# A fused attention, MLP and gate kernel: token tiles 2 to 15 transposed by DMA rather than by TensorE and ScalarE

## The chip, the core, the metric

One core of a Trainium2 chip. The metric is the device time of one execution in microseconds; a kernel is run several times and its median is quoted. All runs told here were in the fast state. "Span" is the length of the one execution that the profiler recorded; it is about 1.8 us shorter than that execution's time. Engines in the profile: PE is TensorE, PEld its weight load, DVE VectorE, ACT ScalarE, POOL GpSimd, SP the queue that issues all DMA.

## The reference, cut

```python
# x: 2048 tokens x 1024, 32 heads of 32, F = 3584, all bf16
xn  = layernorm(x)
q, k, v = split_heads(xn @ wqkv)
s   = concat(softmax(q k^T / sqrt(32)) v) @ wo
g   = silu(gelu(layernorm(xn) @ w1 + b1) @ w2 + b2)    # tanh form of gelu
return x + s * g
```

## The kernel before

The whole block is one program. Attention runs as 512 "units": 8 groups of four heads, times 8 query blocks of 256 tokens, times 8 key pairs of 256. A unit is a score group of 8 matmuls, two exponentials of 128x1024 on ScalarE, 8 matmuls with V, and a row sum by ones-matmuls. All other matmuls (projections, the MLP for 8 chunks of 256 tokens, the output projection) are slipped between the score groups, through the two PSUM banks that attention leaves free. The order of each engine is made when the program is built, by a list scheduler in the kernel itself, with a small cost model (a duration for each instruction, a bandwidth for loads). On the chip every engine then follows its list, whatever really happens.

Start, for each token tile: statistics on VectorE, `pow` and the normalising pass on GpSimd, then the transpose:

```python
def tr_item(t, half=None):                       # eight 128x128 transposes on TensorE ...
    ...
        ins = e.transpose(bankb(b)[:, dc*128:(dc+1)*128], xnb[t % 4][:, dc*128:(dc+1)*128], ident[:])
    ...                                          # ... and a copy out of PSUM on ScalarE
        act(lambda e: e.activation(dst, src(), ACT.Copy), c_act(128 * n), [], W, 0, it)
...
for t in (lo, lo + 1):
    pool(... xnb[t % 4] = xst[t] * rs + nb ...)  # one pass over 128x1024
pro_q += [tr_item(lo), tr_item(lo + 1), k_pair_item(n, False)]
```

First layer of the MLP, one item of 512 columns:

```python
dve(... xb = psum + b1 ...); dve(... sq = xb * xb ...); dve(... ut = (sq + 1/GA) * xb ...)
act(lambda e: e.activation(ut_t[i3][:], ut_t[i3][:], ACT.Tanh, scale=GC * GA), c_act(512), ...)
dve(... h = (ut + 1) * xb ...)
```

Row sums over two units; the first NOPA units make no additions on VectorE and leave the summing to TensorE:

```python
NOPA = 24
def ones_pair(u, pv):
    pa = dve(... PA[u], PA[u+1] = P[.., 0, :] + P[.., 1, :] ...)   # 2048 wide
    pb = dve(... PA[u] += PA[u+1] ...)                             # 1024 wide
    ...
    if u < NOPA or u >= HG * 64 - 2: plan.skip.append(pa)
```

The cost model's view of a load, and of an issue on the queue:

```python
state["bw"] = max(state["bw"], t) + o.nbytes / 210.0     # bytes per ns
return add("SP", fn, 70, 0, R, W, prio, sem=sem, nbytes=nbytes, extra=extra)
```

## Time and profile before

| | before |
|---|---|
| median of 3 | 1062.07 us (1061.9 to 1062.5) |
| span of the profiled run | 1060.2 us |
| first exponential, 15th exponential | 12.7, 45.9 us |
| end of the last exponential | 1046.1 us |
| from there to the end (tail) | 14.1 us |
| 512-wide matmuls after the last exponential | 42 |

The prediction below shows the busy line, the chain and the stretches. Two more views matter later. The first line is the granted TensorE clock in 40 slices of the page; the others are the last pieces of the chain (start, length, instruction).

```profile
PEclk9999999999999999999999999999999999999999
...
1047.59 9.24 PE ps L668 x42
...
1056.86 0.70 DVE w1r L1221
...
1057.58 0.43 DVE w1r L1228
```

The clock is full in nearly all of the span: no slice is under nine tenths, but one stretch of 3.41 us, at 57.65 us, has half the clock. After the last exponential the chain is 42 left-over matmuls of the output projection in one run of 9.24 us, two short operations and a store. That line deserved more attention than it got: work of TensorE is left over when ScalarE has finished.

### The profile page before, as it was taken

The numbers are of one execution on the slowest core, as the hardware profiler recorded it, in microseconds if no ns is written. First come the engines' busy times: TensorE is split into PE (matmuls) and PEld (weight loads), VectorE is DVE, ScalarE is ACT, GpSimd is POOL, SyncE is SP. The second block draws the span as 40 slices with busy tenths as digits, with TensorE's granted clock in tenths as the row PEclk, the third lists the DMA queues.
The fourth block names the chain that finished last, engine by engine and source line by source line (L and its number), as shares of the span: only waits on it lengthen the run. The fifth ranks groups of instructions, "written<-read, shape, count | busy, mean of one in ns | idle before, by whom it ended". The sixth has DMA issues, their size and how long they took to land.

```text
span 1060.2 us, 32647 instructions
## 1 busy us (share of the span) xinstructions
PE 1026.5 (97%) x14502; PEld 643.7 (61%) x14562; DVE 946.9 (89%) x1585; ACT 1028.9 (97%) x1186; POOL 31.2 (3%) x42
## 2 busy tenths in 40 slices
PE   7999999999999999999999999999999999999998
PEld 5756466556665566566665566466665666665443
DVE  8479898999999998899989998999999998978996
ACT  4999999999999999999999999999999999999994
POOL 5500000000000000000000000000000000000000
PEclk9999999999999999999999999999999999999999
DMA  9335166522674466423763476224765776662442
GB/s 268 111 96 158 42 179 190 144 76 71 186 207 126 113 193 196 113 57 112 206 192 105 122 199 195 74 76 121 212 180 151 221 217 190 179 197 70 134 140 87
DMA packets 285798, 156.52 MB, mean 148 GB/s; under 512 B 23642, under 2 KB 276570, under 8 KB 285658
## 3 DMA queue, kind: packets, MB, share of 16 engines
q1 hardware_dynamic: 285658, 154.44, 51.0%
q8 instruction: 114, 1.87, 0.8%
q14 instruction: 26, 0.21, 0.1%
HBM read 142.35 MB, written 12.06 MB: 146 GB/s over the span
## 4 chain that ended last, share of the span: by engine, by line
ACT 93%; PE 4%; DVE 2%; DMA 1%; issue 0%; SPq 0%; POOL 0%; POOLq 0%
ACT P L1067 86%; ACT ut L939 5%; PE ps L668 3%; ACT gw L971 2%; DVE stats L823 1%; DMA hT<-in_A_x_dram 1%; PE ps L663 1%; ACT big L814 0%; PE ps L1058 0%; PE ps L803 0%; DVE yT L911 0%; POOL gw L847 0%; DVE V L740 0%; DVE mv L825 0%; SPq L693 0%
## 5 line engine op out<-in xcount | busy, mean ns | idle before, releaser
L1067 ACT ACTIVATE P<-ps 128x1024 bf16<-128x1024 f32 x1024 | 986.8, 1243 | 5.3 <-PE ps L1058 5.3
L1087 DVE TENSOR_TENSOR PA<-P 128x2048 bf16<-128x2048 bf16 x243 | 294.7, 1215 | 25.4 <-ACT P L1067 24.1
L668 PE MATMUL ps<-yT,w1r 128*128 128x256 bf16 x1792 | 234.9, 275 | 2.3 <-DVE xb L931 1.1
L668 PE MATMUL ps<-w2r,hT 128*128 128x256 bf16 x1792 | 226.9, 273 | 0.3 <-DVE nv L1121 0.2
L668 PEld LDWEIGHTS ps<-yT,w1r 128*128 128x128 bf16 x1792 | 162.1, 98 | 60.5 <-issue 28.6
L668 PEld LDWEIGHTS ps<-w2r,hT 128*128 128x128 bf16 x1792 | 162.2, 98 | 51.0 <-issue 30.5
L1091 DVE TENSOR_TENSOR PA<-PA 128x1024 bf16<-128x1024 bf16 x219 | 147.7, 684 | 1.4
L663 PE MATMUL ps<-P,V 128*32 128x256 bf16 x4096 | 142.8, 274 | 0.6 <-DVE xb L931 0.4
L668 PE MATMUL ps<-big,qk 128*128 128x512 bf16 (+2 forms) x522 | 120.9, 357 | 5.7 <-issue 2.1
L668 PE MATMUL ps<-qk,big 128*128 128x256 bf16 (+1 forms) x723 | 121.2, 305 | 2.5 <-issue 1.3
L663 PEld LDWEIGHTS ps<-P,V 128*32 128x32 bf16 x4096 | 97.7, 96 | 33.1 <-issue 19.6
L1058 PE MATMUL ps<-QKT 32*128 32x256 bf16 x2048 | 101.7, 273 | 7.4 <-ACT P L1067 5.9
L1058 PE MATMUL ps<-qk 32*128 32x256 bf16 x2048 | 101.9, 273 | 6.2 <-ACT P L1067 2.1
L939 ACT ACTIVATE ut<-ut 128x512 f32<-128x512 f32 x112 | 94.5, 855 | 0.0
L668 PEld LDWEIGHTS ps<-qk,big 128*128 128x128 bf16 x736 | 65.3, 98 | 41.5 <-issue 13.3
L931 DVE TENSOR_TENSOR xb<-ps,b1T 128x512 bf16<-128x512 f32 x112 | 76.6, 684 | 13.9 <-PE ps L668 12.6
L941 DVE SCALAR_TENSOR_TENSOR hT<-ut,xb 128x512 bf16<-128x512 f32 x112 | 76.4, 684 | 5.9 <-ACT ut L939 5.2
L668 PEld LDWEIGHTS ps<-big,qk 128*128 128x128 bf16 x568 | 47.7, 98 | 52.4 <-issue 15.6
L1058 PEld LDWEIGHTS ps<-QKT 32*128 32x128 bf16 x2048 | 30.3, 92 | 76.6 <-ACT P L1067 75.9
L937 DVE SCALAR_TENSOR_TENSOR ut<-sq,xb 128x512 f32<-128x512 bf16 x112 | 76.1, 682 | 0.3
L1058 PEld LDWEIGHTS ps<-qk 32*128 32x128 bf16 x2048 | 30.4, 92 | 71.6 <-ACT P L1067 67.4
L663 PE MATMUL ps<-PA,ones 128*32 128x256 bf16 x1068 | 56.0, 274 | 0.3 <-DVE PA L1091 0.3
(75 smaller groups left out, 532.2 us busy)
## 6 DMA issues: line engine op xcount, KB each, us to landing
w1r<-in_B_w_dram SPq DMA_DIRECT2D x112, 512.0 KB, 4.4
w2r<-in_B_w_dram SPq DMA_DIRECT2D x128, 448.0 KB, 4.4
qk<-in_A_wqkv_dram SPq DMA_DIRECT2D x16, 256.0 KB, 3.2
g_scratch<-gw SPq DMA_DIRECT2D x32, 128.0 KB, 3.0
o_scratch<-ot SPq DMA_DIRECT2D x56, 64.0 KB, 2.8
big<-o_scratch SPq DMA_DIRECT2D x28, 128.0 KB, 3.5
hT<-in_A_x_dram SPq DMA_DIRECT2D x10, 256.0 KB, 5.5
qk<-in_A_wqkv_dram SPq DMA_DIRECT2D x4, 512.0 KB, 4.4
```

The source lines that it names most:

```text
L663: ins = e.matmul(dst(j), lhsT=lhsT(j), rhs=rhs(j), start=start, stop=stop, tile_position=(0, 32 * j), skip_group_check=True)
L668: return e.matmul(dst, lhsT=lhsT, rhs=rhs, start=start, stop=stop, skip_group_check=True)
L823: dve(lambda e, t=t, c=c: e.bn_stats(stats[:, t, c, :], xst[t][:, c * 512:(c + 1) * 512]), 600, [XS(t)], [("st", t, c)], 1)
L931: dve(lambda e: e.tensor_tensor(xb_t[i3][:].rearrange("p (k t) -> p k t", k=2), bank(it.bank).rearrange("p (k t) -> p k t", k=2), b1T[:, 2 ...
L937: dve(lambda e: e.scalar_tensor_tensor(ut_t[i3][:], sq_t[p % 2][:], 1.0 / GA, xb_t[i3][:], op0=ALU.add, op1=ALU.mult), c_f32(512), [("sq", ...
L939: act(lambda e: e.activation(ut_t[i3][:], ut_t[i3][:], ACT.Tanh, scale=GC * GA), c_act(512), [("ut", i3)], [("ut", i3)], 1)
L941: dve(lambda e: e.scalar_tensor_tensor(hT[:, hs].rearrange("p k t -> p (k t)"), ut_t[i3][:], 1.0, xb_t[i3][:], op0=ALU.add, op1=ALU.mult), ...
L971: act(lambda e: e.activation(zh_t[zi], z_t[zi], ACT.Tanh, scale=0.5), c_act(512), [("z", zi)], [("zh", zi)], 1)
L1058: ins = e.matmul(bank(b0[j], kk * 256, (kk + 1) * 256), lhsT=QKT[sl][32 * j:32 * j + 32, 1, kb * 128:(kb + 1) * 128], rhs=QKT[sl][32 * j:3 ...
L1067: x = act(lambda e, h=h: e.activation(P[pi][:, 2 * h:2 * h + 2].rearrange("p j k q -> p (j k q)"), ps[:, pr[h] * 1024:(pr[h] + 1) * 1024], ...
L1087: pa = dve(lambda e: e.tensor_tensor(PA_all[:, a0:a0 + 2].rearrange("p u j q -> p (u j) q"), P_all[:, p0:p0 + 2, :, 0, :].rearrange("p u j ...
L1091: pb = dve(lambda e: e.tensor_tensor(PA[a0][:], PA[a0][:], PA[a1][:], op=ALU.add), c_b16(1024), [("PA", a1)], [("PA", a0)], PBPRIO)
```

## The change

The intent: take 14 copies off ScalarE and 112 transposes off TensorE in the start by transposing with DMA, and, in the same edit, make the tanh wider, the matmul chunks finer and the end shorter. The diff also changes nine other constants of the scheduler (GRACE1, GRACE2, HARD, EARLY, RESERVE, GLAST, OLAG, PJC and PJD), which set when it puts which work; no run sets these back alone. The diff cut to its core:

```diff
-NOPA = 24
+NOPA = 0
 ...          # other constants of the scheduler
+FINE = 1          # MLP and V matmuls may be interrupted after each, not after two
+PART = 5
+TD = 2            # tiles from 2 on: DMA transpose
 ...
-                state["bw"] = max(state["bw"], t) + o.nbytes / 210.0
-                o.fin = state["bw"] + 1900.0
+                state["bw"] = max(state["bw"], t) + o.nbytes / 280.0
+                o.fin = state["bw"] + (2600.0 if o.sem.startswith("tp") else 1900.0)
 ...
-            return add("SP", fn, 70, 0, R, W, prio, ...)
+            return add("SP", fn, 430, 0, R, W, prio, ...)
 ...
-            pro_q += [tr_item(lo), tr_item(lo + 1), k_pair_item(n, False)]
+            for t in (lo, lo + 1):
+                if t < TD:
+                    pro_q.append(tr_item(t))
+                else:
+                    add("SP", lambda e, t=t: e.dma_start_transpose(out=xnT[:, :, t * 128:(t + 1) * 128], in_=xnb[t % 4]),
+                        1500, 0, [("xnb", t % 4)], [("xnT", t, h) for h in range(2)], 0, sem=f"tp{t % 4}", nbytes=360000)
+            pro_q.append(k_pair_item(n, False))
 ...          # first w1 loads, later x loads and the third wq/wk load wait for tiles of the start
-            act(lambda e: e.activation(ut_t[i3][:], ut_t[i3][:], ACT.Tanh, scale=GC * GA), c_act(512),
+            act(lambda e: e.activation(ut_t[i2][:], ut_t[i2][:], ACT.Tanh, scale=GC * GA), c_acts(1024),
 ...
-        def ones_pair(u, pv):
+        def ones_four(u, pv):         # additions over four units: one ones-matmul group in place of two
 ...
+                if qb == PART:        # heads 0 to 6 of the last 256 tokens are projected early,
+                    ...               # head 7 alone is left for the end
+                            wo_item(NQB - 1, t2, nh, 0, 7)
```

> **What bounds the kernel now.** I read the page's busy line, then the chain of work that ended last, then stretches of the span, and only then single instructions.
>
> The busy line and the chain, from the page of the kernel before:
>
> ```profile
> PE 1026.5 (97%) x14502; PEld 643.7 (61%) x14562; DVE 946.9 (89%) x1585; ACT 1028.9 (97%) x1186; POOL 31.2 (3%) x42
> ...
> ACT 93%; PE 4%; DVE 2%; DMA 1%; issue 0%; SPq 0%; POOL 0%; POOLq 0%
> ...
> L1067 ACT ACTIVATE P<-ps 128x1024 bf16<-128x1024 f32 x1024 | 986.8, 1243 | 5.3 <-PE ps L1058 5.3
> ```
>
> Two engines stand at 97%, but the chain is ACT for 93% of the span: the 1024 exponentials of the softmax. Their mean of 1243 ns overlaps the neighbour; what one costs is the step from its start to the next start. The cost of the other ACT work shows in this timeline of ACT (start, length, instruction):
>
> ```profile
> 404.62 0.91 ACT L939 ACTIVATE ut<-ut 128x512 f32<-128x512 f32 x1
> 405.14 6.80 ACT L1067 ACTIVATE P<-ps 128x1024 bf16<-128x1024 f32 x7
> 411.58 0.87 ACT L971 ACTIVATE gw<-gw 128x512 f32<-128x512 bf16 x1
> 412.10 4.94 ACT L1067 ACTIVATE P<-ps 128x1024 bf16<-128x1024 f32 x5
> ```
>
> A 512-wide tanh costs 405.14 - 404.62 = 0.52 us. Over the trace the commonest step of an exponential is 0.904 us, the mean 0.915. The stretches show where ACT is not full:
>
> ```profile
> 12.70:46.00 33.30, 30.40 (x350) 24.10 (x349) 25.33 (x67) 26.75 (x29) 26.49 (x32) 1.00 0.65 185
> 46.00:967.00 921.00, 901.04 (x13021) 577.82 (x13067) 834.49 (x1362) 920.08 (x1069) 0.00 (x0) 1.00 0.52 148
> 967.00:1046.10 79.10, 75.42 (x988) 32.10 (x997) 71.01 (x119) 79.08 (x87) 0.00 (x0) 1.00 0.39 123
> 1046.10:1060.20 14.10, 10.56 (x80) 5.00 (x79) 7.41 (x15) 0.00 (x0) 2.31 (x2) 1.00 0.21 75
> ```
>
> (Columns: length, then busy time of PE, PE weight load, DVE, ACT, POOL, clock, DMA.) There are three regimes: a start until 46 us, in which units of attention wait for their token tiles; 1000 us with ACT continuously busy; and a tail of 14.1 us without any ACT. The account of the ACT regime: at 45.94 the 15th exponential starts; 1009 x 0.904 = 912.1, 144 tanh x 0.52 = 74.9 and the last one's 1.25 end at 1034.2. It really ends at 1046.1, so 12 us are small bubbles, nearly all ahead of the first exponential of a unit.
>
> In the start, ACT's copies of transposed tiles alternate with the exponentials:
>
> ```profile
> 33.55 3.77 ACT L814 ACTIVATE big<-ps 128x1024 bf16<-128x1024 bf16 x4 [0.35 <-PE ps L803]
> 37.18 1.97 ACT L1067 ACTIVATE P<-ps 128x1024 bf16<-128x1024 f32 x2
> 38.99 2.00 ACT L814 ACTIVATE big<-ps 128x1024 bf16<-128x1024 bf16 x2
> ```
>
> but POOL, which normalises the tiles, is as full (26.5 of 33.3 us, and 4.2 to 4.75 in each 5 us from 15 to 40). Its pairs of tiles are 3.56 us apart (rows at 20.43 and 23.99), and the last pair ends at 38.2.
>
> **What the skill says.** The Trainium skill, "ScalarE: Activation LUTs", section "What ACT_TABLE_LOAD costs": an ACTIVATE with immediate scale and bias takes 186 ns + 0.833 ns per column, and neighbours overlap by about 93 ns. The step would be 93 + 0.833N: 519.5 ns at N = 512, and the trace has 520. So for a 1024-wide tanh, which no trace here has yet, I estimate 946 ns from that formula. The skill's "DMA: Bandwidth & Descriptors", section "DMA Transpose (X-bar)", limits DMA transposes to 2-byte types and the Sync or Scalar queues; its section "Latency and other measured facts" gives an effective 261 GB/s, so a 256 KB tile is an estimated 1.0 us of transfer. No trace of before has one; plain 256 KB loads in the start needed 5.5 to 7.1 us from issue to landing in a busy queue, 2.6 to 3.2 later. "VectorE: DVE Perf Modes", section "The perf-mode tier table": a bf16 addition of two tensors runs at 2x at most, one from PSUM at 1x. It agrees: 1024-wide bf16 additions step at 0.60 us, 512-wide operations from PSUM at 0.60 us.
>
> **The change, part by part.** The diff holds much more than its title, and the built order of instructions gives the counts.
>
> 1. *DMA transposes.* 112 of 128 TensorE transposes and 14 of 15 full ACT copies go; 14 DMA transposes come. The copies are worth 14 x 0.92 = 12.9 us of ACT, but only what the first eight units wait for counts, since those units need the tiles in order. The new path for the last tile: POOL's train of seven pairs does not change (about 38.2, perhaps half a microsecond later, because three small POOL operations now stand inside it), then issue and landing, which I put at 4.2 us (about 1.0 transfer plus the plain loads' latency plus issue), 1.0 of PE for K, 0.5 of DVE copy with its latency, 0.5 for scores: 38.4 + 4.2 + 1.0 + 0.5 + 0.5 = 44.6, against 45.94. Gain about 1.4 us, not 12.9.
> 2. *Tanh over pairs.* 112 + 32 of 512 become 56 + 16 of 1024: 144 x 0.52 = 74.9 against 72 x 0.946 = 68.1. Gain 6.8 us, all on the path.
> 3. *Finer chunks.* MLP and V matmuls may be interrupted after each (0.109 us) rather than after two (0.218), so a ready score group waits less. Many bubbles of 80 to 150 ns are of that size. I halve the 12 us of bubbles: gain 6.
> 4. *Tree of additions over four units.* Ones-matmuls fall from 1276 to 1000, 69 groups of four at about 0.11 to 0.17: 8 to 11 us of PE. DVE: 2048-wide additions 243 to 254, 1024-wide 219 to 266: 11 x 1.135 + 47 x 0.60 = +40.7; pairing in the MLP takes away about 56 x 0.07 twice and 16 x 0.07, 9 us. Net +32 us, some 92% of its span. PE and DVE stay beside ACT, so the path gains nothing.
> 5. *The last 256 tokens.* Heads 0 to 6 of the output projection are now summed before attention ends. Before, after 1046.1: the last PV and ones to 1047.4, the norm, then matmuls until 1056.86 in groups 1.73 apart, the last two DVE operations to 1058.0, and 2.2 of store. After: one ones-group less (-0.4), the first remaining matmul 3.0 after ACT's end, four of them 0.22 apart, four 0.60 reads of PSUM and two 0.60 additions on DVE (POOL does two beside it), the store: 3.0 + 0.6 + 3.6 + 2.2 = 9.4. Gain 4.7 us.
>
> Sum: 44.6 + 912.1 + 68.1 + 1.25 + 6 = 1032.1 as ACT's end, + 9.4 = 1041.5 of span. The measured time was 1.9 over the span before: **1043.4 us**, a gain of 18.7, or 1.8%.
>
> **The rivals.** (a) *PE takes over.* PE is busy 901 of 921 us in the middle and 75.4 of 79.1 later, and the chain before still had ten left-over matmuls after ACT's end. If PE can't be compressed with ACT, only its own savings of 8 to 11 count, the 28 early matmuls cost 6 of it, and the time is about 1050. Against it: 20 us of PE's lost time stand just before score groups, where PE itself waits for ACT to free a bank. (b) *DVE takes over.* At 92% and with additions of 1.1 us that cannot be interrupted, reads of the two flexible PSUM banks may come late, PE stalls, and bubbles grow instead of halving: about 1050 to 1055. Against it: the schedule drops an addition that is late and lets TensorE sum instead. (c) *The transposes are slow.* All go through one queue, four buffers hold normalised tiles; at 2.5 us each from 16 us on, the 14 end at 51 and the time is about 1054. Against it: the 261 GB/s. (d) *The transfers are so quick and the copies mattered so much* that units follow at 40 us, and bubbles nearly vanish: 1035.
>
> **Range and chances.** The sum has two soft terms, bubbles (-4 to +8) and the start (-4 to +5), and rival (a). I give 1034 to 1053. The border of 2% is 1041.2, just under my figure, so the chance of faster is 0.40, within 2% 0.57, slower 0.03.
>
> **What would show it.** Right: ACT's 15th exponential near 44.6 with ACT idle some 17 us in the start; tanh steps of 0.946; ones-matmuls 1000; bubbles of the middle near 6 us; from ACT's end to the end 9.4. The chain must stay over 90% ACT. Wrong: a share of PE or DVE in the chain well above the 4% and 2% of before; matmuls of the projection left over after the last exponential; or POOL waiting for transposes to free its buffers.

## The result, and the profile after

| | before | after |
|---|---|---|
| median | 1062.28 us (4 runs, 1061.90 to 1063.47) | 1072.01 us (4 runs, 1070.72 to 1073.35) |
| span of the profiled run | 1060.2 | 1071.0 |
| 15th exponential starts | 45.9 | 51.7 |
| last exponential ends | 1046.1 | 1052.8 |
| tail | 14.1 | 18.2 |

The ratio is 1.0090, 95% interval 1.0072 to 1.0107: slower, and outside the predicted range. A ratio here is the mean time of one kernel's fast runs over that of the other's of the same rounds, so not quite the ratio of the medians that stand beside it. The medians of the kernel before differ a little from call to call (1060.5 to 1062.3), so kernels of different calls are compared by their ratios to it. Within a call its executions are of two sorts, about 1.2 us apart (1060.5 and 1061.7, say), with a mean clock of 1.000 and of 0.998.

The page of the kernel after: busy line, clock, chain.

```profile
PE 1024.5 (96%) x14174; PEld 633.6 (59%) x14174; DVE 983.4 (92%) x1523; ACT 1011.3 (94%) x1100; POOL 34.2 (3%) x42
...
PEclk8899999999999999999999999999999999999999
...
ACT 78%; PE 17%; DVE 3%; DMA 1%; POOL 1%; issue 0%; DVEq 0%
```

ScalarE's busy time fell by 17.6 us and the kernel became 10 us slower. The first two slices no longer have the full clock, and the chain has gone from ACT 93%, PE 4% to ACT 78%, PE 17%.

Its stretches (length, then busy time of PE, weight load, DVE, ACT, POOL, then clock, DMA share, GB/s):

```profile
12.70:46.00 33.30, 23.82 (x201) 16.96 (x199) 29.22 (x67) 11.63 (x12) 27.96 (x32) 0.84 0.84 167
46.00:967.00 921.00, 897.66 (x12812) 572.69 (x12810) 855.15 (x1284) 912.11 (x993) 1.70 (x1) 1.00 0.54 153
967.00:1052.90 85.90, 82.13 (x1046) 33.35 (x1044) 76.55 (x126) 84.54 (x92) 0.00 (x0) 0.98 0.35 109
1052.90:1071.00 18.10, 11.30 (x66) 4.95 (x64) 13.56 (x24) 0.00 (x0) 2.28 (x2) 0.91 0.16 58
```

In the start, where the transposes and copies went, PE does 201 matmuls rather than 350, and at a clock of 0.84. The middle is not continuously busy on ACT any more (912 of 921 us). What fills the start is visible in PE's timeline, first of the kernel after, then of the kernel before (start, length, instruction, and in brackets the idle time ahead of it and its releaser):

```profile
19.98 1.89 PE L709 MATMUL ps<-qk,big 128*128 128x256 bf16 x8 [3.84 <-DMA big<-gw]
21.66 1.86 PE L709 MATMUL ps<-big,qk 128*128 128x256 bf16 x8
```

```profile
19.15 1.04 PE L668 MATMUL ps<-big,qk 128*128 128x256 bf16 x8
```

PE waits 3.84 us for a transposed tile and then takes 1.86 us for eight matmuls that took 1.04: half the clock is granted for 3.41 us from 19.92 us on. The transposes in the table of DMA issues (last number: median us from issue to landing):

```profile
big<-gw SPq DMA_TRANSPOSE x10, 3.1
big<-yT SPq DMA_TRANSPOSE x4, 3.2
```

They are not slow to land. The wide tanh, in ACT's timeline, costs what was predicted, 401.64 - 400.70 = 0.94 us to the next start:

```profile
400.70 1.34 ACT L1040 ACTIVATE gw<-gw 128x1024 f32<-128x1024 bf16 x1
401.64 6.81 ACT L1138 ACTIVATE P<-ps 128x1024 bf16<-128x1024 f32 x7
```

A new sort of loss in the middle, in two stretches of 3.41 us of the kernel after that follow each other (columns as above):

```profile
101.84:105.25 3.41, 1.04 (x40) 0.80 (x40) 3.34 (x5) 3.41 (x5) 0.00 (x0) 1.00 0.69 195
105.25:108.66 3.41, 3.41 (x76) 2.65 (x64) 1.48 (x3) 2.07 (x3) 0.00 (x0) 0.50 0.00 0
```

PE waited 2.37 us while ACT made two tanh of 0.95 us in a row; in the next 3.41 us it is granted half the clock, and ACT in its turn is busy for only 2.07. Another loss is a weight load that lands later than the schedule supposed:

```profile
909.07 0.49 PE L709 MATMUL ps<-yT,w1r 128*128 128x256 bf16 x3 [1.71 <-DMA w1r<-in_B_w_dram]
```

The end of the chain:

```profile
1053.74 9.62 PE ps L709 x44
...
1063.38 0.69 DVE V L1279
1064.07 2.39 DVE w1r L1279 x4
1066.46 0.84 DVE V L1282
1067.30 0.60 DVEq L1369
1067.91 0.60 DVE w1r L1284
```

The left-over matmuls are there as before, in a run of 44 (the last of which is the first of the four for head 7), and the short operations for the last 256 tokens now follow them one after another.

### The profile page after: what moved, and what is told of

It is laid out like the page before. It is cut to its first block, busy times and chain, and to the rows that moved or that the text cites. A ratio compares the mean times of both kernels' runs of the same rounds, so it can differ in the third digit from the quotient of the medians.

```text
span 1071.0 us, 31821 instructions
## 1 busy us (share of the span) xinstructions
PE 1024.5 (96%) x14174; PEld 633.6 (59%) x14174; DVE 983.4 (92%) x1523; ACT 1011.3 (94%) x1100; POOL 34.2 (3%) x42
## 4 chain that ended last, share of the span: by engine, by line
ACT 78%; PE 17%; DVE 3%; DMA 1%; POOL 1%; issue 0%; DVEq 0%
ACT P L1138 72%; PE ps L709 11%; ACT ut L1004 4%; PE ps L1129 3%; PE ps L704 3%; DVE ut L862 1%; DMA w1r<-in_B_w_dram 1%; ACT gw L1040 1%; POOL gw L894 0%; POOL lnp L915 0%; DMA hT<-in_A_x_dram 0%; DVE lnp L880 0%; DVE w1r L1279 0%; DVE mv L864 0%; DVE xb L989 0%
## 5 line engine op out<-in xcount | busy, mean ns | idle before, releaser
L1138 ACT ACTIVATE P<-ps 128x1024 bf16<-128x1024 f32 x1024 | 962.1, 1199 | 34.4 <-PE ps L1129 33.0
L1159 DVE TENSOR_TENSOR PA<-P 128x2048 bf16<-128x2048 bf16 x254 | 307.6, 1213 | 21.1 <-ACT P L1138 19.3
L704 PE MATMUL ps<-P,V 128*32 128x256 bf16 x4096 | 146.4, 275 | 0.5 <-ACT P L1138 0.4
L1164 DVE TENSOR_TENSOR PA<-PA 128x1024 bf16<-128x1024 bf16 x209 | 143.0, 691 | 1.2
L709 PE MATMUL ps<-big,qk 128*128 128x512 bf16 (+2 forms) x568 | 134.4, 369 | 2.7 <-DMA big<-gw 1.1
L709 PE MATMUL ps<-qk,big 128*128 128x256 bf16 (+1 forms) x736 | 128.2, 313 | 5.1 <-DMA big<-gw 3.8
L709 PEld LDWEIGHTS ps<-qk,big 128*128 128x128 bf16 x736 | 67.4, 100 | 47.2 <-issue 17.3
L709 PEld LDWEIGHTS ps<-big,qk 128*128 128x128 bf16 x568 | 50.7, 102 | 54.6 <-issue 15.2
L1004 ACT ACTIVATE ut<-ut 128x1024 f32<-128x1024 f32 x56 | 68.8, 1228 | 0.0
L1002 DVE SCALAR_TENSOR_TENSOR ut<-hT,xb 128x1024 f32<-128x1024 bf16 x56 | 68.2, 1217 | 0.0
L1213 DVE STREAM_TRANSPOSE nt<-ps 128x256 f32<-128x256 f32 x64 | 28.7, 448 | 24.9 <-PE ps L704 24.4
```

The source lines that it names most:

```text
L704: ins = e.matmul(dst(j), lhsT=lhsT(j), rhs=rhs(j), start=start, stop=stop, tile_position=(0, 32 * j), skip_group_check=True)
L709: return e.matmul(dst, lhsT=lhsT, rhs=rhs, start=start, stop=stop, skip_group_check=True)
L1002: dve(lambda e, r=r: e.scalar_tensor_tensor(ut_t[i2][:, r], h[:, r], 1.0 / GA, xb[:, r], op0=ALU.add, op1=ALU.mult), c_f32(r.stop - r.star ...
L1004: act(lambda e: e.activation(ut_t[i2][:], ut_t[i2][:], ACT.Tanh, scale=GC * GA), c_acts(1024), [("ut", i2, 0), ("ut", i2, 1)], [("ut", i2, ...
L1138: x = act(lambda e, h=h: e.activation(P[pi][:, 2 * h:2 * h + 2].rearrange("p j k q -> p (j k q)"), ps[:, pr[h] * 1024:(pr[h] + 1) * 1024], ...
L1159: add2.append(dve(lambda e, p0=p0, a0=a0: e.tensor_tensor(PA_all[:, a0:a0 + 2].rearrange("p u j q -> p (u j) q"), P_all[:, p0:p0 + 2, :, 0 ...
```

## The account that the experiments are judged by

From each trace I take: the start of the 15th exponential; 1009 further exponentials at their commonest step of 0.904 us, 912.1 us; the tanh at 0.520 us (512 wide) or 0.947 us (1024 wide); what ACT's steps exceed these by, split into small bubbles (under 250 ns each) and stalls (over); the last exponential; and the tail. The parts add up to the span within 1 us. "Left" counts the 512-wide matmuls that start after the last exponential has ended, the last four included. These columns come from one profiled execution each. How much they vary by chance is seen in pairs of runs whose kernels differ only in the order of the last few items: between e4 and e6 the 15th exponential differs by 0.3 us and the stalls by 0.4, between e5 and e9 by 0.5 and 1.7.

| run | ratio to before (95%) | median us | 15th exp | tanh | bubbles | stalls | tail | left |
|---|---|---|---|---|---|---|---|---|
| before | | 1062.3 | 45.9 | 74.9 | 11.0 | 1.1 | 14.1 | 42 |
| after | 1.0090 (1.0072-1.0107) | 1072.0 | 51.7 | 68.2 | 11.1 | 8.7 | 18.2 | 48 |
| e1 | 1.0075 (1.006-1.009) | 1068.8 | 49.3 | 68.2 | 9.9 | 10.7 | 17.3 | 44 |
| e2 | 1.0102 (1.0087-1.0117) | 1071.8 | 48.1 | 74.9 | 10.8 | 3.8 | 19.3 | 65 |
| e3 | 1.0071 (1.0053-1.0088) | 1067.9 | 48.8 | 68.2 | 10.6 | 7.1 | 17.3 | 44 |
| e4 | 1.0040 (1.0023-1.0057) | 1064.8 | 50.2 | 68.2 | 11.0 | 3.3 | 17.3 | 44 |
| e5 | 1.0001 (0.9986-1.0016) | 1061.4 | 47.0 | 68.2 | 11.4 | 2.3 | 17.3 | 44 |
| e6 | 1.0027 (1.001-1.0044) | 1064.2 | 50.5 | 68.2 | 11.0 | 3.7 | 15.3 | 44 |
| e7 | 1.0100 (1.0085-1.0115) | 1072.1 | 49.7 | 68.2 | 11.3 | 9.6 | 18.2 | 47 |
| e8 | 0.9969 (0.9954-0.9983) | 1057.9 | 45.6 | 16.6 | 10.2 | 32.2 | 37.9 | 149 |
| e9 | 0.9979 (0.9964-0.9994) | 1059.2 | 46.5 | 68.2 | 11.1 | 4.0 | 15.4 | 44 |
| e10 | 0.9992 (0.9977-1.0007) | 1060.0 | 48.7 | 68.2 | 11.0 | 3.5 | 15.4 | 44 |
| e11 | 1.0015 (0.9994-1.0035) | 1062.0 | 46.3 | 68.2 | 12.4 | 0.7 | 18.0 | 54 |
| e12 | 1.0015 (1.0000-1.0030) | 1063.5 | 45.7 | 68.2 | 11.4 | 3.7 | 20.6 | 71 |
| e13 | 1.0163 (1.0147-1.0179) | 1078.6 | 45.9 | 74.9 | 11.0 | 0.8 | 31.4 | 123 |
| e14 | 1.0036 (1.0023-1.005) | 1064.5 | 45.5 | 74.9 | 10.4 | 4.1 | 14.6 | 45 |
| e15 | 0.9983 (0.9971-0.9996) | 1059.8 | 46.9 | 68.2 | 11.1 | 3.0 | 14.6 | 45 |

## The experiments

The theory after the result: TensorE is as full as ScalarE, so ScalarE's saving is not a gain by itself; what TensorE loses in the start comes back at the end; and three things of the change do harm beside its title (additions in the start, loads planned too fast, the order of the end). The main rival: ScalarE alone sets the time, as its 93% of the chain says, and the loss is the DMA transposes' alone.

### The parts of the start (e1, e2, e3)

e1 is the changed kernel with the transposes given back to TensorE and ScalarE.

```diff
-TD = 2
+TD = 16
```

> The changed kernel with one constant set back, so that all 16 tiles are again transposed by TensorE and copied by ACT; all other parts of the change stay. Theory A (the DMA path and the half clock of an idle TensorE cost the start about 5.7 us): the 15th exponential starts near 46 instead of 51.7, the clock stays at 1.00 in the start, and the time falls by 4 to 7 us to about 1066. Theory B (the loss is in the rest of the change): 1071 to 1073 as the changed kernel.

Measured: 1.0075, start 2.4 us earlier than after, which is between the two theories. Most of the loss stays: in this kernel the transposes in the title are not its main cause. Whether giving them back gains anything is not settled, since the interval overlaps that of the changed kernel.

e2 does the opposite: the kernel before with the DMA transposes, and with the throttled and gated loads and the planned bandwidth of the start, and nothing else of the change.

```diff
+            for t in (lo, lo + 1):
+                add("SP", lambda e, t=t: e.dma_start_transpose(...), 1500, 0, ...)
-            pro_q += [tr_item(lo), tr_item(lo + 1), k_pair_item(n, False)]
+            pro_q.append(k_pair_item(n, False))
 ...          # loads as in the change
```

> The kernel before with the transposing path of the change alone: DMA transposes of tiles 2 to 15, the throttled loads and the order of loads that come with them; softmax sums, tanh and tail as before. Theory A: the start lasts to about 51 us instead of 46, half-clock stretches appear before 46 us, and the time is 1066 to 1069. Theory B: 1061 to 1063, the start as before.

Measured: 1.0102, slower than either theory expected. The 15th exponential is 2.1 us later, yet the kernel is 11 us slower; the second layer of the MLP ends at 976.7 us rather than 964.0, 65 matmuls are left over rather than 42, and the tail is 5.2 us longer. So a delay of TensorE's work is still there at the end. This fits a full TensorE; it could also be a worse order. It weighs on what follows: e2 has neither the additions in the start nor the faster planned loads after 60 us nor the new end, and loses as much as the whole change. What it loses by was not taken apart.

e3 is the changed kernel with 28 idle-filling matmuls in the start, to hold TensorE's clock.

```diff
+            for t in (lo, lo + 1):
+                it = _Item("pro", 1)
+                for _ in range(2):
+                    it.chunks.append(add("PE", ... full(e, bank(it.bank), ident[:], ...) ..., extra=(xnop[t],)))
+                pro_q.append(it)
```

> The changed kernel with two dummy 512-wide matmuls per DMA-transposed tile (28 in all, 6 us of TensorE at full clock, about what the removed transposes took), their results never read. If the half clock in the start comes from TensorE being idle, the clock in 12.7 to 46 us rises from 0.84 towards 1.00 and the 15th exponential comes 1 to 3 us sooner, time 1069 to 1071. If the half clock has another cause or does not matter for the path, the start stays at 51.7 and the time at 1072 or above.

Measured: 1.0071; half clock in the start 6.8 us instead of 13.7, the 15th exponential 2.9 us earlier. That points to a cost of the lower clock in the start, but the interval of the ratio overlaps that of the changed kernel, so a gain is not settled; and e5 below starts its 15th exponential at 47.0 with 13.7 us of half clock in the start.

### Loads planned too fast (e4)

```diff
-                state["bw"] = max(state["bw"], t) + o.nbytes / 280.0
+                state["bw"] = max(state["bw"], t) + o.nbytes / (280.0 if t < 60000 else 210.0)
```

> The changed kernel, but its scheduler counts on 210 bytes per ns of load bandwidth after 60 us, as the kernel before does, rather than 280. Theory C: the two waits of TensorE for first-layer weights (0.7 and 1.7 us) and what follows from them come from loads that land later than planned; with the old figure they vanish and the time falls by 2 to 3 us to about 1069.5. Rival: such waits merely move, 1071 to 1073.

Measured: 1.0040, more than half of the loss gone, and more than theory C expected. PE's two waits for weights of the first layer (2.4 us together in the kernel after) are absent, stalls fall from 8.7 to 3.3 us. The edit changes no transfer, only the order in which the scheduler puts the work. It is the base of the next three runs.

### Additions in the start (e5)

```diff
-NOPA = 0
+NOPA = 24
```

> The changed kernel with loads planned at 210 bytes per ns after 60 us (the base of this call, 1064.8 us before), and in addition the first 24 units of attention are summed by TensorE as in the kernel before, so that VectorE makes no softmax additions in the start. Theory A (additions of 1.3 to 1.5 us in the start delay GpSimd's normalising and the casts of K, which hold up the units): the 15th exponential starts 2 to 4 us earlier than the 50.2 of the base, near 47, and the time falls to about 1062. Rival B (the start is set by the landing of transposed tiles and half-clocked matmuls alone): the 15th exponential stays within 1 us of 50.2 and the time within 1 us of 1064.8.

Measured: 1.0001, the 15th exponential 3.2 us earlier than in its base e4, at 47.0: as theory A expected. The reason is in the timelines of GpSimd and VectorE. The kernel after, GpSimd and then VectorE:

```profile
35.73 2.27 POOL L894 TENSOR_SCALAR gw<-w2r,lnp 128x1024 bf16<-128x1024 bf16 x1
...
38.57 1.19 POOL L894 TENSOR_SCALAR gw<-w2r,lnp 128x1024 bf16<-128x1024 bf16 x1
...
39.95 2.24 POOL L894 TENSOR_SCALAR gw<-w2r,lnp 128x1024 bf16<-128x1024 bf16 x1
```

```profile
37.18 1.35 DVE L1164 TENSOR_TENSOR PA<-PA 128x1024 bf16<-128x1024 bf16 x1
...
39.98 1.22 DVE L1159 TENSOR_TENSOR PA<-P 128x2048 bf16<-128x2048 bf16 x1
...
41.23 1.49 DVE L1164 TENSOR_TENSOR PA<-PA 128x1024 bf16<-128x1024 bf16 x1
```

GpSimd's last pass in e4, the base of this run (the first line), and its last two in this run, without additions:

```profile
41.73 1.19 POOL L894 TENSOR_SCALAR yT<-w2r,lnp 128x1024 bf16<-128x1024 bf16 x1
```

```profile
36.82 1.20 POOL L894 TENSOR_SCALAR gw<-w2r,lnp 128x1024 bf16<-128x1024 bf16 x1
...
38.56 1.20 POOL L894 TENSOR_SCALAR yT<-w2r,lnp 128x1024 bf16<-128x1024 bf16 x1
```

A normalising pass that takes 1.20 us alone takes 2.24 to 2.27 where an addition runs beside it, and the additions, 0.60 us apart elsewhere, become 1.35 and 1.49 us long. The Trainium skill, "SBUF — State Buffer", section "Who interferes with whom", says that a VectorE instruction with two SBUF inputs contends with GpSimd's reads and that the loser is blocked, not slowed; the trace agrees: the addition of 39.98 us ends at 41.20, the pass that began at 39.95 ends only at 42.19, 0.99 us later, and the addition that began at 41.23 ends at 42.72, 0.53 us after that pass. With the additions gone GpSimd's last tile is ready at 39.8 us rather than 42.9 in e4 (44.3 in the kernel after).

### The order of the end (e6, e15)

```diff
+        wq_ = plan.queues["wo"]
+        wq_[-6:] = wq_[-4:] + wq_[-6:-4]        # e15: wq_[-7:] = wq_[-4:] + wq_[-7:-4]
```

> The same base; only the order of the last output projections changes: the four matmuls of head 7 for the last 256 tokens come two items (16 matmuls, 3.5 us) earlier, so that what VectorE, GpSimd and the store do for them lies beside the remaining left-over matmuls. Theory A (the tail is long because the four operations of the last tokens follow one another after a queue of 44 left-over matmuls): the tail falls from 17.3 us to about 14, the time to about 1061.5. Rival B (the tail is only the left-over matmuls and a fixed end): tail and time within 1 us of the base.

Measured: tail 15.3 rather than 17.3, part of what theory A expected. The time is 1.4 us less by the ratios, but the intervals of e4 and e6 overlap, so only the tail of the trace is shown. The operations for the last tokens now lie beside left-over matmuls.

> As e9, with the four head-7 matmuls three items earlier rather than two, so that the operations of VectorE and GpSimd for the last 256 tokens begin 1.8 us sooner. If these still are the end (in e9 the last matmul started 10.1 us after the last exponential and 5.3 us passed from there to the end), the tail falls from 15.4 to 14.4 and the time from 1059.2 to 1058. If the store or the left-over matmuls are the end, it stays within 0.5 us of e9.

e15 is made from e9 below. Measured: the tail fell to 14.6 as expected, the time did not (0.9983 against 0.9979). Inconclusive: the difference is inside the intervals.

### Which engine is full (e7, e8, e12, e13, e14)

e7 takes 14 us of TensorE work away from e4, by leaving out 128 second-layer matmuls. (The result was meant to be wrong; the comparison's tolerance accepted it.)

```diff
-                        fs = [f for f in range(f0, f0 + FINE) if f < 7]
+                        fs = [f for f in range(f0, f0 + FINE) if f < (6 if r >= 2 else 7)]
+                        if not fs:
+                            continue
```

> The same base, wrong result on purpose: 128 of the 1792 second-layer matmuls are left out, 14 us of TensorE at 0.109, and nothing of ScalarE. Theory A (TensorE is co-bound with ScalarE: what it lacks in the start comes back as left-over matmuls): the last second-layer matmul ends some 14 us earlier than 964, fewer than 30 rather than 44 wide matmuls follow the last exponential, and the time falls by 4 us or more, to 1060. Rival B (ScalarE sets the end, the left-over matmuls only wait for the norms of the last groups and for free banks): the second layer ends earlier, but still some 44 matmuls are left over and the time stays within 1.5 us of 1064.8.

Measured: 1.0100, slower than its base by 0.6%, which neither theory expected. Left-over matmuls are 47 where the base has 44, as rival B said. Where the time went, in PE's timeline and in a stretch behind it (length, busy PE, weight load, DVE, ACT, POOL, clock):

```profile
910.71 0.40 PE L1131 MATMUL ps<-qk 32*128 32x256 bf16 x8 [2.37 <-ACT P L1140]
```

```profile
912.25:915.66 3.41, 3.41 (x68) 2.01 (x60) 2.48 (x4) 2.91 (x4) 0.00 (x0) 0.50 0.09 21
```

With less to do, PE waits longer in one piece for ACT, is granted half its clock for the next 3.41 us or more, and then ACT waits for PE. Half clock comes four times after 900 us and before the end; ACT's stalls grow from 3.3 to 9.6 us in all. Less work on the engine, but not less time.

e8 takes ScalarE's first-layer tanh out of the kernel before, 58 us (the result is wrong on purpose, and was found wrong).

```diff
-            act(lambda e: e.activation(ut_t[i3][:], ut_t[i3][:], ACT.Tanh, scale=GC * GA), c_act(512),
-                [("ut", i3)], [("ut", i3)], 1)
```

> The kernel before, wrong result on purpose: the 112 tanh of the first layer are left out, 112 x 0.52 = 58 us of ScalarE's work, and nothing else. Theory A (TensorE and its order are nearly as full as ScalarE): the time falls by less than 20 us, ScalarE's idle stretches grow by 40 us or more, and the chain of work moves to PE. Rival B (ScalarE alone sets the time, as the chain of 93% suggests): the time falls by 45 to 58 us to 1003 to 1017, and tanh made cheaper by 6.8 us should have shown in full.

Measured: 3.8 us faster by the medians of this call. The chain of the run, and its last stretch:

```profile
ACT 63%; PE 31%; DVE 4%; DMA 1%; issue 0%; POOL 0%; POOLq 0%
```

```profile
1017.90:1055.80 37.90, 34.15 (x187) 15.74 (x189) 22.53 (x42) 0.00 (x1) 2.30 (x2) 1.00 0.56 174
```

Of 58 us, 31 became stalls of ACT (theory A expected 40) and 24 became tail, in which 149 matmuls are left over and ACT is idle. Rival B, ScalarE alone, is out by a factor of more than ten. The edit takes nothing but tanh out, but the scheduler makes a new order of it: 16 second-step additions of VectorE are dropped (203 rather than 219), and TensorE makes 64 more ones-matmuls in their place.

e12 is the disputed part alone: the kernel before with the tanh over pairs of items, as the change has it, 72 of 1024 columns.

```diff
-            act(... ut_t[i3] ..., ACT.Tanh, scale=GC * GA), c_act(512), ...)     # 112 and 32 times
+            act(... ut_t[i2] ..., ACT.Tanh, scale=GC * GA), c_acts(1024), ...)   # 56 and 16 times
```

> The kernel before with one part of the change alone: tanh over pairs of items, 72 of 1024 columns in place of 144 of 512, and the VectorE work beside it in pairs; chunks of two matmuls as before. The prediction's step 2 says -6.7 us, all on the path: ratio 0.9937, tail 14. Theory A (ScalarE's time is worth 4 of 58 us, as the run without tanh showed, since TensorE is as full): tanh sums to 68.2 instead of 74.9, but the time stays within 1.5 us of the kernel before or rises, because more left-over matmuls follow the last exponential or because PE waits longer for pairs.

Measured: tanh 68.2 instead of 74.9, the last exponential ends at 1042.1 instead of 1046.1, and the kernel is not faster (1.0015). Its last stretch:

```profile
1042.10:1062.70 20.60, 16.99 (x109) 7.94 (x109) 11.37 (x22) 0.01 (x1) 2.31 (x2) 1.00 0.39 128
```

71 matmuls follow the last exponential rather than 42; 29 x 0.217 = 6.3 us, and the tail is 6.5 us longer. Of the 6.7 us saved, 2.6 became stalls, and the 4.0 by which ScalarE still ended sooner were more than used up by TensorE's remaining work. Two reservations. The profiled run was the slowest of the five (1064.5; two took 1061.1 and 1061.4), so none of the five is faster than the kernel before at its fastest, 1060.6, but the lines show the worst of them. And the run is not ScalarE's saving alone: the scheduler dropped 17 additions of VectorE (202 rather than 219), so TensorE made 68 more ones-matmuls, which run four at a time (2 to 5 ns from one start to the next); at the prediction's 0.11 to 0.17 us a group I estimate 2 to 3 us. The order, too, is another.

e13 and e14 add and take 14 us of TensorE work in the kernel before, with ScalarE's work untouched: 128 second-layer matmuls made twice, or left out.

```diff
                         fs = [f for f in (f0, f0 + 1) if f < 7]
+                        if f0 == 6 and r >= 2:
+                            fs = [6, 6]          # e14: continue
```

> The kernel before, wrong result on purpose: 128 second-layer matmuls are made twice, 128 x 0.109 = 14 us of TensorE, spread over the middle; ScalarE's and VectorE's work is untouched. Theory A (TensorE is as full as ScalarE and has no slack left): the time rises by 10 to 20 us, nearly all of it as more left-over matmuls after the last exponential (42 becomes 90 or more). Rival B (ScalarE sets the time and TensorE's 3% are slack): the 14 us vanish in TensorE's waits, the time rises by less than 4 us.

Measured: 1078.6 against 1060.8, 17.8 us for 14 us of work. The last exponential ends where it did (1045.8), and then:

```profile
1047.13 26.67 PE ps L668 x123
```

TensorE has no slack that this order can use: the work came back in full, and 3.8 us more. (This result, too, passed the comparison.)

> The kernel before, wrong result on purpose: the same 128 matmuls are left out, 14 us less of TensorE. Theory A' (both engines are full, so less of the one alone gains little, and the last groups must wait for the last exponentials in any case): the time moves by less than 5 us either way and some 40 matmuls are still left over. Rival (TensorE alone sets the time): 10 us or more faster. If it comes out slower, as in the changed kernel, TensorE's waits with windows of half clock behind them will show in the trace.

Measured: 3.7 us slower, with 45 left over: theory A'. Before its end TensorE falls to half clock twice, at 1008.5 and 1039.2, and 2.7 of its 4.1 us of stalls stand behind these two. So TensorE alone is not the bound either. The 45 left-over matmuls of a kernel with 14 us less work also show that some 40 of them are no measure of a full TensorE: its second layer ends 12 us earlier (952.1 rather than 964.0), and they still come after the last exponential. My reading is that both engines are full: more work on TensorE costs all of its length, less work on either one alone gains at most 3.8 us, and here even costs. Two things are not shown. No run takes work from both at once, which should gain if this is so; and every run has a new order, made by a scheduler that does not know the real times, so a poor order is a rival that these runs do not exclude.

### The repairs together (e9, e10, e11)

e9 is the changed kernel with three repairs: e4, e5 and e6.

> The changed kernel with three repairs together: loads planned at 210 bytes per ns after 60 us, no softmax additions in the first 24 units, the four head-7 matmuls two items earlier. If the gains of the runs that had them one by one (-3.4 us for the additions, -1.4 for the order of the end) add, the time is about 1060, ratio to before 0.998 to 1.000, 15th exponential near 47.0, tail 15.3. If they overlap (what the start gains is lost again as waits), it stays at 1061.4 or above.

Measured: 0.9979, interval below 1. The ratios fall step by step: 1.0090, with slower planned loads 1.0040, without early additions 1.0001, with the other end 0.9979. The first two steps are clear of the intervals, the last is not. It is the lowest ratio of a kernel with a right result, ahead of the kernel before by 0.2%; e10 and e15 are inside its interval.

e10 is e9 with the start of the kernel before (TensorE transposes, loads neither throttled nor gated).

```diff
-TD = 2
-XF = 3
-XA = 8
+TD = 16
+XF = 2
+XA = 16
...                  # gates of the w1 and wq/wk loads removed, 210 bytes per ns and 70 ns an issue throughout
```

> As the run before, but with the start of the kernel before: all tiles transposed by TensorE and ScalarE, loads as then, neither throttled nor gated. Theory A (the DMA transposes cost TensorE its clock in the start: 13.7 us at half clock in the run with no early additions, none before 57 us in the kernel before; and TensorE is co-bound): no half clock in the start, 15th exponential near 46, time 2 to 3 us below the run with the DMA transposes. Rival B (once the additions are out of the start the DMA transposes do no harm, and the 13 us of ScalarE copies that they save count): the time is 1 us or more above it.

Measured: 0.9992. Its start is worse than expected (15th exponential 48.7, 6.8 us of half clock from 14.1 on), so theory A failed; but the difference from e9, 0.13%, is inside the intervals. With the rest repaired, the DMA way is 1.4 us ahead in the means, and no sure gain.

e11 is e9 with chunks of two matmuls.

```diff
-FINE = 1
+FINE = 2
```

> As e9, but first-layer, second-layer and V matmuls may again be interrupted only after two of them (0.218 us), not after each (0.109). If the finer chunks of the change are worth what the prediction gave them, the small bubbles (ScalarE steps less than 250 ns above their floor) go from 11.4 us to some 17 and the time rises by 4 to 6 us. Rival: the small bubbles do not come from the grain of the chunks; they stay within 1.5 us of 11.4, and the time moves only by what the other order of the work brings, within 2 us.

Measured: small bubbles 12.4 against 11.1 us: the rival. The finer grain is worth 1.3 us of bubbles, not 6; the median rose by 2.8 us, more than the rival's 2. The profiled run, the fastest of six, has 10 more matmuls after the last exponential and a tail 2.6 us longer, so what was lost seems to lie in the order, and its runs scatter widely (1060.6 to 1066.2).

## Why the prediction was wrong, point by point

Its own sum, term by term, in us of the span:

| term | predicted | measured |
|---|---|---|
| 15th exponential | 44.6 | 51.7 |
| 1009 exponentials | 912.1 | 912.1 |
| tanh | 68.1 | 68.2 |
| last exponential | 1.25 | 1.1 |
| small bubbles | 6 | 11.1 |
| stalls | 0 | 8.7 |
| tail | 9.4 | 18.2 |
| span | 1041.5 | 1071.0 |

1. *The start, +7.1.* The failed step is "POOL's train of seven pairs does not change (about 38.2...)". It ended at 44.3, +5.9, in the main because the change let VectorE's additions into the start (NOPA from 24 to 0, a line of the diff that I read past) and they block GpSimd. e5 shows it for 3.1 us: without the additions the train ends at 39.8 rather than at the 42.9 of its base e4. The other 2.8 (1.4 between the kernel after and e4, 1.4 that stay in e5) are open. The rest of the path, put at 6.2 us from GpSimd's last tile to the 15th exponential, measured 7.4; the last tile landed in 3.2 us of it, where the prediction had 4.2 for issue and landing, so the landing was not the trouble.
2. *Tanh, right in size* (68.2 for 68.1). "Gain 6.8 us, all on the path" failed in its last words. e12 made that saving on the kernel before and got nothing; e8 made one of 58 us and got 4. The chain of waits named ACT for 93%, because at nearly every step it was ACT that released last; it does not say how far behind the next engine is.
3. *Bubbles, +5.* "I halve the 12 us of bubbles" rested on their size alone (80 to 150 ns, that of a chunk). They stayed at 11.1; e11: the grain is worth 1.3 us.
4. *The tree of additions.* The counts came as predicted (254 and 266 additions, 1000 ones-matmuls), and DVE's busy time rose by 36.5 us (predicted 32). "PE and DVE stay beside ACT, so the path gains nothing" missed that the additions also run in the start, point 1.
5. *The tail, +8.8.* The failed step is "the first remaining matmul 3.0 after ACT's end". The four matmuls come behind 44 left-over ones; the first of them is done 10.5 us after. From there to the end it took 7.6 us where 6.4 were predicted; e6 hides 2 us of that. The prediction speaks of ten left-over matmuls in the kernel before; the chain of that kernel has 42.
6. *Stalls, +8.7,* had no term. Most go with loads planned faster than they land (e4 takes 5.4 us of them away); in the traces others stand in half-clocked windows after waits of PE.

Rival (a), "PE takes over", came nearest in mechanism, not in size (it said 1050), and the argument against it was wrong: the 20 us that PE was said to lose ahead of score groups (the page has 13.6, of which 8.0 are put down to ACT) looked like slack, but e13 shows that 14 us of new work cost 17.8. Two of the three signs named for "wrong" appeared as named: PE's share of the chain rose (4% to 17%), and matmuls of the projection were left over (48; but the kernel before already had 42, and e14 has 45). The third, GpSimd waiting for transposes, did not.

Settled: new work on TensorE costs its full length; in the changed kernel the planned loads (e4) and, on top of that, the additions in the start (e5) cost time clear of the intervals; the order of the end (e6) costs 2.0 us of tail in the trace, not clear in the time; and with all three undone the loss is gone. Open: why e2, which has none of the three, loses 11 us; what the other constants of the scheduler do; whether work taken from both engines at once would gain; whether the DMA transposes gain anything (e9 against e10); and how much of the loss by half clock a better order could avoid.

## What to carry to other kernels

A chain that is 93% one engine does not say that this engine's saving is the gain: look for work that another engine has left over when the first one ends, and add a known amount of work to each engine in turn, one run each (done here for TensorE alone; that ScalarE is full is read from its 920 busy us of 921). Read a diff for its constants as carefully as for its title; much of the harm here came from two of them (NOPA and the planned bandwidth). In a kernel whose order is fixed when it is built, a wrong figure in the cost model costs time on the chip though no instruction changed; and an edit meant for one engine can move work of another, so count the instructions of every engine after it.

## What the Trainium skill lacked or had wrong

- "TensorE: Matmul & The Clock Gate", section "HAM oscillation — how this bites in real kernels", gives the rule in the abstract as no PE-idle gaps over about 3.4 us. Here one wait of 2.37 us (at 104.2 us of the kernel after, and at 910.7 us of e7) was followed by 3.41 us at clock 0.50, and so were two waits of 1.44 and 0.47 us close together (1028.5 and 1030.3 us of the kernel after). The clock records of all 17 traces change in steps of 3.41 us; I counted PE's idle time in each such window between 10 us and the last exponential. In 38 windows at full clock that were followed by half clock PE had idled 1.26 to 3.41 us, in 31 of them over 1.74; no window with over 1.74 us idle was followed by full clock and none under 1.26 by half; between these both occurred.
- No page that I found gives the time that issuing a DMA transpose of a 128x1024 tile from SBUF to SBUF takes on its queue: here 1.23 to 1.35 us for 11 of the 14 in the kernel after and 1.46 to 2.57 for the other three, while the landing, 3.1 to 3.2 us from issue in the median (2.7 to 5.2), was no slower than the plain loads of the same size in the start (4.6 us).
- No page says how to tell that two engines are full at once: here 58 us less on ScalarE gained 3.8 us, and 14 us more on TensorE cost 17.8.
